# Tiles passed through memory in column blocks, with other queues and other places for the statistics, in a spectral and dense network on one core

## The chip, the core and the metric

One NeuronCore of a Trainium2 chip runs the whole program in one launch. It has five engines with a queue each: TensorE (PE, matrix products), VectorE (DVE), ScalarE (ACT), GpSimd (POOL) and SyncE (SP, which here only issues DMAs). DMAs can be issued from the queues of SyncE, ScalarE and GpSimd; a queue is worked off in order, so an issue that waits for a semaphore holds up all that stands behind it. The metric is the time on the device in microseconds (us).

## The reference

Four layers follow each other on a sequence of 2048 rows (tokens) with 1024 columns: A, B, A, B. Each one normalises its input along the columns and adds its result to it.

```python
def _layernorm(x, axis=-1, eps=1e-5):
    m = jnp.mean(x, axis=axis, keepdims=True)
    v = jnp.var(x, axis=axis, keepdims=True)
    return (x - m) / jnp.sqrt(v + eps)
...
    def _A_ref(x, w_r, w_i):
        X = rfft2(x)                      # over rows and columns, 2048 x 1024
        X = X * (w_r + 1j * w_i)
        return irfft2(X).astype(bfloat16)

    def _B_ref(x, w1, b1, w2):
        h = einsum("bsd,df->bsf", x, w1) + b1      # 1024 -> 3584
        act = h * tanh(softplus(h))                # Mish
        return einsum("bsf,fd->bsd", act, w2)      # 3584 -> 1024

    x = x + _A_ref(_layernorm(x), A_w_r, A_w_i)
    x = x + _B_ref(_layernorm(x), B_w1, B_b1, B_w2)
    x = x + _A_ref(_layernorm(x), A_w_r, A_w_i)
    x = x + _B_ref(_layernorm(x), B_w1, B_b1, B_w2)
```

## The kernel before, in words

The sequence stays in on-chip memory as 16 tiles of 128 rows (`XS`, tile `j` = rows `128 j` to `128 j + 127`). Layer A is written as products with tables of sines and cosines; its first stage (`s1`, matmuls at L635) wants the normalised sequence in another layout, `XR`: one partition for each pair of tile `j` and column block `h` (eight blocks of 128 columns), and in each partition 128 rows by 128 columns. Layer B computes both dense products with a scheme of seven block products instead of eight (Strassen's, in Winograd's form), for a pair of token groups at a time: tiles 0 to 7, and tiles 8 to 15.

A tracker turns reads and writes of named buffers into semaphore waits, and every engine executes its instructions in the order in which the program emits them. The order of the work is thus the order of the Python code; there is no scheduler. Buffers are places in one arena; a new buffer in an old place waits for the old one's readers and writers.

Layer B runs in this order, with the parts that matter here:

- The first dense product of tiles 8 to 15 is not finished when the first group's second product begins. `products(0, ...)` is the second product of the first half of the tokens. It has seven stages (n = 0 to 6), each a block product for four tiles (t = 0 to 3), at L1268; after each (n, t) the function `extra` is called. The two halves of a weight block lie in the slots `PB[n][k]`. Where the layer is not the last, five weight loads are issued just ahead of `products(0, ...)` (L1500, `load_w2`): three from SyncE's queue, two from GpSimd's. Differences of weight blocks (`w2_sum`, L1260) are made on VectorE out of pairs of these loads. `B21` is the second half of the block that stage 1 multiplies with (`PB[1][1]`).
- `stats_act(j)` takes the mean and the sum of squares of tile `j` on ScalarE, in two passes of L453 over 1024 columns. Where the layer is not the last, stages 5 and 6 of `products(0, ...)` each call it four times, for tiles 0 to 7 in all, whose new values stages 1 to 6 have just written (L1319).
- `quads(range(14), ...)` is the first dense product of the second half of the tokens: 14 passes of seven block products, 28 matmuls in a pass, at L1186. ScalarE copies the first of them out of PSUM (L574), VectorE adds others to that copy (L1191), and ScalarE applies Mish (L1196). Matmuls that go on accumulating in the bank of the first product wait for L574. The weights of pass n come from one of three slots; a slot is filled (`fill_slot`) from SyncE's queue when its pass is done, for passes 3 to 5 with four sums on GpSimd behind the load (L1081), for later passes from sums kept in memory (`w1s`). After each pass n, `after(n)` is called. It holds the arithmetic that turns sums into scales (`sums_to_mv`, `scales`, eleven small VectorE instructions), the normalisation of tiles 0 to 7 (`apply`, L524) and their stores to memory (`xn_store`), issued on GpSimd.
- `products(1, ...)` is the second product of the second half of the tokens. Its stages come in the order `BACK`, in which the last two stages finish tiles 8 to 11 (n = 5) and 12 to 15 (n = 6) one after the other. `extra` there normalises each finished tile and passes it on; at (3, 3), where the place of `XR` has become free, it issues the loads of tiles 0 to 7 (`xr_load`).
- After the last tile TensorE runs 24 matmuls without use (`spin`, L652), and layer A begins with `s1`, which needs all of `XR`'s first 64 rows of every tile before its first group (eight groups), and the rest before the ninth.

A normalised tile goes to `XR` in one of two ways. Through memory: `xn_store` writes the tile as it is (128 rows of 2 KB) to `xn_d[j]`, issued on GpSimd for tiles 0 to 7 and on ScalarE for 8 to 12; `xr_load`, on GpSimd, reads it back in runs of 256 B, so that the eight column blocks land on eight partitions. Directly: `xr_direct` copies each column block from on-chip memory to its partition, with one DMA for each block. Tiles 13 and 14 are copied with eight DMAs each, in turn from SyncE and GpSimd; tile 15 with sixteen (two halves of the rows), in turn from SyncE, GpSimd and ScalarE.

Of the kernel before, what the change touches and what calls it, by code (L numbers as in the profile page):

```python
# [7 lines left out]
P = 128  # L8
BF = dt.bfloat16
# [171 lines left out]
class KB:  # L181
# [123 lines left out]
    def build(self):  # L305
        nc = self.nc
        tabs = make_tables()
        con = {k: nc.inline_tensor(to_bf16_bits(v), name=f"c_{k.lower()}") for k, v in tabs.items()}
        self.con = {k: v.ap().bitcast(BF) for k, v in con.items()}
        self.con["IDF"] = nc.inline_tensor(np.eye(P, dtype=np.float32), name="c_idf").ap()  # L310
        self.u_d = nc.dram_tensor("u_scratch", (8, P, 16, P), BF, kind="Internal").ap()
        self.w_d = nc.dram_tensor("w_scratch", (8, P, 2, 2, 512), BF, kind="Internal").ap()
        self.w1s_d = nc.dram_tensor("w1s_scratch", (14, P, 3584), BF, kind="Internal").ap()
        self.w2s_d = nc.dram_tensor("w2s_scratch", (4, P, 14, 512), BF, kind="Internal").ap()
        self.xn_d = nc.dram_tensor("xn_scratch", (16, P, self.D), BF, kind="Internal").ap()
        from contextlib import ExitStack
        with ExitStack() as es:
            def sb(name, shape, dtype=BF):
                return es.enter_context(nc.sbuf_tensor(name, [P] + shape, dtype))

            sb("PAD0", [64])
            self.XS = sb("XS", [16, self.D])
            self.IDENT = sb("IDENT", [P])
            self.M = sb("M", [P])
            self.MT = sb("MT", [P])
            self.FD = sb("FD", [5 * 512])
            self.BD = sb("BD", [13 * P])
            self.B1 = sb("B1", [self.NF], F32)
            self.B1h = sb("B1h", [self.NF])
            self.BN = sb("BN", [16, 12], F32)  # L330
            self.MV = sb("MV", [16, 2], F32)
            self.RS = sb("RS", [4, 16], F32)
            self.EPS = sb("EPS", [32], F32)
            sb("PAD1", [32])
            self.PS = es.enter_context(nc.psum_tensor("PS", [P, 8, 512], F32))
            self.PSb = self.PS[:].bitcast(BF)
            self.arena_bytes = nc.sbuf_bytes_remaining // 64 * 64 - 64
            self.ARENA = es.enter_context(nc.sbuf_tensor("ARENA", [P, self.arena_bytes // 2], BF))
            self.r_bank = [Res(f"bank{i}") for i in range(8)]
            self.r_xs = [Res(f"XS{i}") for i in range(16)]  # L340
            self.r_mv = [Res(f"MV{i}") for i in range(16)]
            self.r_rs = [Res(f"RS{i}") for i in range(16)]
            self.r_ident, self.r_m, self.r_mt, self.r_fd, self.r_bd = (Res(n) for n in ("id", "m", "mt", "fd", "bd"))
            self.r_b1, self.r_eps, self.r_warm = Res("b1"), Res("eps"), Res("warm")
            self.r_ud = [Res(f"ud{i}") for i in range(8)]
            self.r_ud7 = [Res(f"udh{i}") for i in range(2)]
            self.r_wd = [Res(f"wd{i}") for i in range(8)]
            self.r_w1d = [Res(f"w1d{i}") for i in range(14)]
            self.r_w2d = [[Res(f"w2d{i}{k}") for k in range(2)] for i in range(4)]
            self.r_xnd = [Res(f"xnd{i}") for i in range(16)]  # L350
            self.npair = 0
            self.W1_OFF = self.arena_bytes - 4 * 4096
            self.layout()
            self.prologue()
            self.layer_A(0)
            self.layer_B(0, last=False)
            self.layer_A(1)
            self.layer_B(1, last=True)
            self.dma_wait_all()
            for p in (self.pe, self.dve, self.act, self.sp, self.pool):  # L360
                p.sem = es.enter_context(nc.semaphore(name=f"sem_{p.name}"))
            for d_ in self.dsems.values():
                d_.sem = es.enter_context(nc.semaphore(name=d_.name))
            self.block = es.enter_context(nc.Block())
            self.flush()

    def layout(self):
        K = 1024
        self.o = dict(XR=0, Z=0, X=12 * K, T=20 * K, YK=28 * K, V=40 * K, JT=48 * K, M0=49 * K, IDF=49 * K + 256, RT=50 * K,
                      JUNK=51 * K, WR=54 * K, YS=96 * K, UT=64 * K, MN=64 * K, Y=96 * K, XN=128 * K, U=128 * K,  # L370
                      FT=140 * K, BT=144 * K + 512, WT=self.W1_OFF)
        self.ob = dict(A=4 * K, XT1=60 * K, XT0=120 * K, XT2=104 * K, XT3=112 * K, W2=68 * K, JUNK=54 * K, TS=128 * K, XN2=140 * K,
                       SUMS=[0, 2 * K, 96 * K, 98 * K, 100 * K], P1=60 * K, X7=96 * K, W=120 * K, XN12=136 * K, JUNK2=0,
                       WS=self.arena_bytes - 21 * K)
        assert 149 * K <= self.W1_OFF and 144 * K <= self.ob["WS"], (149 * K, self.W1_OFF)

# [151 lines left out]

    def xn_store(self, j, b):
        b.unread = False  # L530
        prog = self.act if j >= 8 else self.pool
        self.dma(prog, self.xn_d[j], b.ap, f"xw{prog.name}{b.res.name[2:]}", reads=[b.res], writes=[self.r_xnd[j]])

    def open_xr(self):
        self.XR = self.alloc("XR", self.o["XR"], [P, P])
# [3 lines left out]
        self.r_xr = [halves[0], halves[0], halves[1], halves[1]]  # L539

    def xr_load(self, j):
        self.dma(self.pool, self.XR.ap[row_of(j, 0):row_of(j, 7) + 1:4, :, :], self.xn_d[j].rearrange("n (h l) -> h n l", l=P), f"xl{j % 4}",
                 reads=[self.r_xnd[j]], parts=self.r_xr[1:3])

    def xr_direct(self, j, b, parts, queues):
# [539 lines left out]
    def layer_B(self, li, last):  # L1085
# [411 lines left out]
        self.xn_buf = [self.alloc(f"XN{i}", self.ob["XN12"] + i * 2048, [self.D]) for i in range(2)] + self.xn_out  # L1497
        w2 = {}
        if not last:
            for name, k, slot, prog in (("B12", 0, "Q1", sp), ("B22", 0, "Q3", pool), ("B21", 1, "R0", sp), ("B12", 1, "Q2", pool),  # L1500
                                        ("B22", 1, "Q4", sp)):
                w2[slot] = load_w2(name, k, slot, prog)
            PB[1][1] = w2["R0"]
        else:
            load_b(STD, 1, 1)
            self.fill_slot(ws[2], 2)
# [28 lines left out]
        def extra(n, t):  # L1535
            if n == 0:
                self.stats_act(12 + t)
            if not last:
                own_sums(n, t)
            if (n, t) == (1, 3):  # L1540
                self.sums_to_mv(12, 4)
                self.scales(12, 4)
                normal(12)
                for j in (13, 14, 15):
                    xn[j] = self.apply(j)
            if (n, t) == (2, 2):
                for j in (13, 14, 15):
                    transposed(3, j - 12, xn[j], act, (6, 7, 0)[j - 13])
            turn(2)
            if (n, t) == (4, 3) and not last:  # L1550
                ws[2:] = self.open_slots("WS", self.ob["WS"], 2)
                self.fill_slot(ws[2], 2)
            if n > 4 and not last:
                self.stats_act(4 * n - 20 + t)
            if (n, t) == (5, 3):
                ws[0:2] = self.open_slots("WS", self.ob["WS"], 0, 1)
                for i in range(2):
                    self.fill_slot(ws[i], i)
                token_sums(1, last=False)
            if (n, t) == (6, 1):  # L1560
                B.update(token_sums(1))
        products(0, self.ob["WS"], STD, extra, last)
        order = [ws[n % 3] for n in range(14)]
        assert not turning
        stages = STD if last else BACK
        self.xn_out = self.xn_out + [self.alloc(f"XN{i}", self.ob["XN2"] + i * 2048, [self.D]) for i in range(2)]

        def after(n):
            if n + 3 < 14:
                self.fill_slot(order[n + 3], n + 3)  # L1570
            if 3 <= n < 7:
                load_b(stages, (n - 3) // 2, (n - 3) % 2)
            if not last:
                if n in (0, 3):
                    self.sums_to_mv(4 * (n // 3), 4)
                    self.scales(4 * (n // 3), 4)
                for j in ((), (0, 1), (2, 3), (), (4, 5), (6, 7))[n] if n < 6 else ():
                    self.xn_store(j, self.apply(j, out=True))
        quads(list(range(14)), order, B, after, lead)
        if not last:  # L1580
# [4 lines left out]
        def extra(n, t):  # L1585
# [8 lines left out]
            if n >= 5:  # L1594
# [1 line left out]
                self.stats_second(j, 0, False)  # L1596
                self.root(j, 1)
                b = self.apply(j, out=True)
                if j < 13:
                    self.xn_store(j, b)  # L1600
                if 8 < j < 14:
                    self.xr_load(j - 1)
                if j > 12:
                    self.xr_direct(j, b, j - 13 or 1, (sp, pool, act)[:2 + j // 15])
        products(1, self.ob["XT2"], stages, extra)
        if not last:
            self.spin(24, 7)
# [38 lines left out]
```

## Time and profile before

| what | value |
|---|---|
| time, median of 3 runs | 949.83 us (949.08 to 951.77) |
| span of the profiled execution | 949.6 us (its time 951.46 us) |
| mean granted TensorE clock | 0.982 |
| TensorE busy | 880.0 us, 93% |
| VectorE busy | 624.5 us, 66% |
| ScalarE busy | 429.1 us, 45% |
| GpSimd busy | 167.4 us, 18% |
| moved by DMA | 174.21 MB, mean 183 GB/s |

The profile is one execution. A line of a group or of the timeline names a source line (L453), the engine, the operation and what it writes and reads; a line of waits names who waited, for whom, how long in total, how often, and the longest. The clock is the share of full speed that the TensorE throttle granted. The first layer A and the first layer B fill the span up to about 490 us, the transition between B and the second A lies at 490 to 504 us, and the rest repeats A and B without a layer behind it. The edited parts lie at 229 us (weight loads), 293 to 362 us (statistics, normalisation and stores of tiles 0 to 7) and 454 to 504 us (loads of tiles 0 to 7, and tiles 8 to 15).

### The profile page before, as it was taken

Reading aid. Unit: us, or ns where it says so; the run is one execution under the profiler, and the core shown is the slowest. Engines: PE = TensorE matmul, PEld = TensorE weight load, DVE = VectorE, ACT = ScalarE, POOL = GpSimd, SP = SyncE. Lnnn points to the kernel's source line nnn. Section 1 sums busy time; section 2 is a strip of 40 time slices with the busy share of each in tenths; the row PEclk is TensorE's granted clock in tenths of the full one; section 3 lists DMA queues with packets and bytes.
Section 4 is the critical chain, followed back from the end, with each engine's and each line's share of the span. In section 5 each row is a group of like instructions: output and inputs, shape, how many; then the busy total and the mean of one; then the engine's idle time right before and its main releaser. Section 6 shows DMA issues by size and latency. Waiting matters only on the chain.

```text
span 949.6 us, 13503 instructions
## 1 busy us (share of the span) xinstructions
PE 880.0 (93%) x5473; PEld 471.9 (50%) x5473; DVE 624.5 (66%) x973; ACT 429.1 (45%) x623; POOL 167.4 (18%) x196
## 2 busy tenths in 40 slices
PE   0799699999999799999986996999999999999998
PEld 0577486444444344444435774864444444444443
DVE  7698468686789485557854874646846665555374
ACT  7798475457104655520006984845551005553000
POOL 3922004951005360010341200000000000000000
PEclk9999989999999899999998998999999999999999
DMA  9969853667775288354970697533245634831443
GB/s 287 275 212 303 206 132 128 224 235 196 263 252 182 100 287 343 112 199 155 213 170 17 203 223 195 181 106 115 87 145 175 215 144 155 303 125 60 172 132 114
DMA packets 149583, 174.21 MB, mean 183 GB/s; under 512 B 68480, under 2 KB 127952, under 8 KB 149520
## 3 DMA queue, kind: packets, MB, share of 16 engines
q1 hardware_dynamic: 134416, 123.83, 42.8%
q0 software_dynamic: 12208, 46.54, 14.9%
q10 hardware_dynamic: 2896, 2.97, 1.1%
q8 instruction: 43, 0.70, 0.3%
q14 instruction: 20, 0.16, 0.1%
HBM read 129.47 MB, written 40.37 MB: 179 GB/s over the span
## 4 chain that ended last, share of the span: by engine, by line
PE 75%; DMA 8%; DVE 8%; ACT 5%; SPq 1%; POOL 1%; issue 1%; ACTq 0%; DVEq 0%; POOLq 0%
PE PS L1268 29%; PE PS L1186 25%; PE PS L1148 9%; PE PS L799 2%; ACT ARENA L453 2%; PE PS L725 2%; PE PS L824 2%; PE PS L1020 2%; DMA ARENA<-w2s_scratch 1%; DMA ARENA<-in_B_w_dram 1%; PE PS L1109 1%; DMA ARENA<-c_bt 1%; DMA ARENA<-w1s_scratch 1%; SPq L250 1%; DMA ARENA<-u_scratch 1%
## 5 line engine op out<-in xcount | busy, mean ns | idle before, releaser
L1268 PE MATMUL PS<-ARENA 128*128 128x512 bf16 x1568 | 340.4, 379 | 2.0 <-DMA ARENA<-in_B_w_dram 1.9
L1186 PE MATMUL PS<-ARENA 128*128 128x512 f16 (+1 forms) x1232 | 270.8, 382 | 6.4 <-ACT ARENA L574 5.0
L1268 PEld LDWEIGHTS PS<-ARENA 128*128 128x128 bf16 x1568 | 153.2, 98 | 187.1 <-DMA ARENA<-in_B_w_dram 2.4
L1191 DVE TENSOR_TENSOR ARENA<-PS,ARENA 128x512 f32<-128x512 f32 x220 | 151.9, 691 | 99.2 <-PE PS L1186 90.9
L1186 PEld LDWEIGHTS PS<-ARENA 128*128 128x128 bf16 x1232 | 120.7, 98 | 155.2 <-ACT ARENA L574 5.4
L1196 ACT ACTIVATE ARENA<-ARENA,B 128x512 bf16<-128x512 f32 x132 | 95.2, 721 | 68.9 <-DVE ARENA L1191 62.6
L574 ACT ACTIVATE ARENA<-PS 128x512 f32<-128x512 f32 (+2 forms) x82 | 61.1, 745 | 118.7 <-PE PS L1186 95.8
L1148 PE MATMUL PS<-ARENA 128*128 128x256 bf16 (+1 forms) x576 | 87.6, 310 | 0.2
L1081 POOL TENSOR_TENSOR ARENA<-ARENA 128x512 bf16<-128x512 bf16 x56 | 71.5, 1277 | 81.0 <-DVE ARENA L524 59.9
L453 ACT ACTIVATE ARENA<-XS 128x1024 bf16<-128x1024 bf16 x52 | 54.8, 1054 | 41.3 <-DVE XS L1319 37.2
L1148 PEld LDWEIGHTS PS<-ARENA 128*128 128x128 bf16 x576 | 55.7, 99 | 27.1 <-DVE ARENA L1114 0.9
L1293 DVE TENSOR_TENSOR ARENA<-ARENA 128x3584 bf16<-128x3584 bf16 x32 | 63.9, 2017 | 0.0
L1319 DVE TENSOR_TENSOR XS<-PS,ARENA 128x512 bf16<-128x512 f32 x52 | 35.7, 689 | 38.6 <-PE PS L1268 38.2
L1152 ACT ACTIVATE ARENA<-PS,B 128x256 bf16<-128x256 f32 (+1 forms) x72 | 38.4, 542 | 36.1 <-PE PS L1148 35.7
L1311 DVE TENSOR_TENSOR ARENA<-PS,ARENA 128x512 f32<-128x512 f32 x48 | 33.0, 688 | 31.8 <-PE PS L1268 31.4
L1196 ACT ACTIVATE ARENA<-PS,B 128x512 bf16<-128x512 f32 x44 | 30.2, 687 | 19.1 <-PE PS L1186 19.1
L1307 DVE TENSOR_TENSOR ARENA<-ARENA,XS 128x512 f32<-128x512 f32 x52 | 36.7, 731 | 0.6
L1163 DVE TENSOR_TENSOR ARENA<-ARENA 128x2048 f16<-128x2048 bf16 x16 | 25.3, 1581 | 17.6 <-PE PS L1148 17.3
L799 PE MATMUL PS<-ARENA 128*128 128x256 bf16 x256 | 32.4, 273 | 4.2 <-DVE ARENA L788 3.2
L472 DVE BATCH_NORM_STATS2 BN<-XS 128x6 f32<-128x512 bf16 x52 | 32.7, 671 | 4.6 <-DMA XS<-in_A_x_dram 4.5
L777 ACT ACTIVATE ARENA<-PS 128x1024 bf16<-128x1024 f32 x32 | 33.4, 1074 | 4.5 <-PE PS L773 4.5
L444 ACT ACTIVATE RS<-MV,EPS 128x1 f32<-128x1 f32 (+2 forms) x11 | 3.3, 296 | 71.0 <-DVE MV L565 70.3
(98 smaller groups left out, 833.9 us busy)
## 6 DMA issues: line engine op xcount, KB each, us to landing
ARENA<-in_B_w_dram SPq DMA_DIRECT2D x30, 896.0 KB, 6.6
ARENA<-w1s_scratch SPq DMA_DIRECT2D x30, 896.0 KB, 4.7
ARENA<-w2s_scratch SPq DMA_DIRECT2D x24, 896.0 KB, 6.8
ARENA<-in_B_w_dram SPq DMA_DIRECT2D x26, 512.0 KB, 5.3
w1s_scratch<-ARENA POOLq DMA_DIRECT2D x14, 896.0 KB, 4.3
u_scratch<-ARENA SPq DMA_DIRECT2D x14, 512.0 KB, 3.4
ARENA<-u_scratch SPq DMA_DIRECT2D x14, 512.0 KB, 5.9
w2s_scratch<-ARENA POOLq DMA_DIRECT2D x8, 896.0 KB, 5.0
```

The source lines that it names most:

```text
L453: self.op(act, lambda e, i=i, f=f: e.activation(junk.ap, x, f, accum_out=sums[:, i:i + 1]), reads=[self.r_xs[j]], writes=[junk.res], parts ...
L574: fn = (lambda e: e.activation(dst, src, ACT.Copy)) if scale is None else \
L799: fns.append(lambda e, c=c, part=part: e.matmul(ps[:, c * 256:(c + 1) * 256], yk.ap[:, part, c * P:(c + 1) * P], t[:, (128, 0)[part]:(384, ...
L1081: self.op(self.pool, lambda e, dst=A(dst), x=A(x), y=A(y), op=op: e.tensor_tensor(dst, x, y, op), reads=[b.res] + list(after), writes=[b.rs])
L1148: fns.append(lambda e, db=db, bank=bank, fl=fl: e.matmul(PS[:, bank, 0:w], wb.ap[:, db, fl * P:(fl + 1) * P], x.ap[:, db, tok], start=(db ...
L1152: self.op(act, lambda e, bank=bank, ft=ft, at=at: e.activation(at[:, tok], PS[:, bank, 0:w], ACT.Mish, bias=self.B1[:, ft:ft + 1]), reads= ...
L1186: self.group([lambda e, db=db: e.matmul(PS[:, bank, :], A[:, db, :], mov[:, db, :], start=(start and db == 0), stop=(db == 3), skip_group_ ...
L1191: self.op(dve, lambda e: e.tensor_tensor(dst.ap, PS[:, bank, :], x.ap, ALU.add), reads=[self.r_bank[bank], x.res], writes=[dst.res])
L1196: self.op(act, lambda e: e.activation(at, src, ACT.Mish, bias=self.B1[:, ft:ft + 1]), reads=[res, self.r_b1], writes=[ra])
L1268: self.group([lambda e, i=i, k=k, b=PB[n][k].ap: e.matmul(PS[:, bank, :], ap[:, i, t * P:(t + 1) * P], b[:, i - 7 * k, :], start=(start an ...
L1293: self.op(dve, lambda e: e.tensor_tensor(ap[dst][:, f, :], ap[x][:, f, :], ap[y][:, f, :], op), reads=part(x, k) + part(y, k), writes=part ...
L1307: self.op(dve, lambda e: e.tensor_tensor(a[t], a[t], x, ALU.add), reads=[rx], writes=[r[t]])
```

## The change

The change has four parts; only the first layer B executes them, since the last one has no layer behind it.

1. The scratch `xn_d` is laid out by column blocks: for each tile, eight blocks of 128 rows by 128 columns. `xn_store` scatters a tile into it (1024 runs of 256 B) and is always issued on GpSimd. `xr_load` is issued on SyncE and reads eight runs of 32 KB, one for each partition of `XR`.
2. Tiles 13 and 14 go through memory, too: stores for tiles 8 to 14, and the load of tile j - 1 behind the store of tile j. Only tile 15 is copied directly, in two halves, in turn from GpSimd, ScalarE and SyncE.
3. The ScalarE statistics of tiles 0 to 3 move from stage 5 of `products(0, ...)` to stage 6, those of tiles 4 to 7 from stage 6 into `quads`, after passes 1 to 4. The scales of tiles 0 to 3 follow after pass 4 (before: 0), of 4 to 7 after pass 7 (before: 3); normalisation and stores of two tiles each after passes 5, 6, 8 and 9 (before: 1, 2, 4 and 5). The buffer into which ScalarE writes the values that nobody reads gets a place that is free in `quads` (`JUNK3`).
4. Of the five weight loads ahead of `products(0, ...)`, `B21` is issued first on SyncE (before: second, behind `B12`).

```diff
-        self.xn_d = nc.dram_tensor("xn_scratch", (16, P, self.D), BF, kind="Internal").ap()
+        self.xn_d = nc.dram_tensor("xn_scratch", (16, 8, P, P), BF, kind="Internal").ap()
...
     def xn_store(self, j, b):
         b.unread = False
-        prog = self.act if j >= 8 else self.pool
-        self.dma(prog, self.xn_d[j], b.ap, f"xw{prog.name}{b.res.name[2:]}", reads=[b.res], writes=[self.r_xnd[j]])
+        self.dma(self.pool, self.xn_d[j].rearrange("h n l -> n h l"), b.ap.rearrange("n (h l) -> n h l", l=P), f"xw{b.res.name[2:]}",
+                 reads=[b.res], writes=[self.r_xnd[j]])
...
     def xr_load(self, j):
-        self.dma(self.pool, self.XR.ap[row_of(j, 0):row_of(j, 7) + 1:4, :, :], self.xn_d[j].rearrange("n (h l) -> h n l", l=P), f"xl{j % 4}",
+        self.dma(self.sp, self.XR.ap[row_of(j, 0):row_of(j, 7) + 1:4, :, :], self.xn_d[j], f"xl{j % 4}",
                  reads=[self.r_xnd[j]], parts=self.r_xr[1:3])
...
-            for name, k, slot, prog in (("B12", 0, "Q1", sp), ("B22", 0, "Q3", pool), ("B21", 1, "R0", sp), ("B12", 1, "Q2", pool),
+            for name, k, slot, prog in (("B21", 1, "R0", sp), ("B12", 0, "Q1", sp), ("B22", 0, "Q3", pool), ("B12", 1, "Q2", pool),
                                         ("B22", 1, "Q4", sp)):
...
-            if n > 4 and not last:
-                self.stats_act(4 * n - 20 + t)
+            if n == 6 and not last:
+                self.stats_act(t)
...
+        self.junk = self.alloc("JUNK3", self.ob["JUNK3"], [self.D])
...
             if not last:
-                if n in (0, 3):
-                    self.sums_to_mv(4 * (n // 3), 4)
-                    self.scales(4 * (n // 3), 4)
-                for j in ((), (0, 1), (2, 3), (), (4, 5), (6, 7))[n] if n < 6 else ():
+                if 0 < n < 5:
+                    self.stats_act(3 + n)
+                if n in (4, 7):
+                    self.sums_to_mv(4 * (n // 7), 4)
+                    self.scales(4 * (n // 7), 4)
+                for j in {5: (0, 1), 6: (2, 3), 8: (4, 5), 9: (6, 7)}.get(n, ()):
                     self.xn_store(j, self.apply(j, out=True))
...
                 b = self.apply(j, out=True)
-                if j < 13:
+                if j < 15:
                     self.xn_store(j, b)
-                if 8 < j < 14:
+                if j > 8:
                     self.xr_load(j - 1)
-                if j > 12:
-                    self.xr_direct(j, b, j - 13 or 1, (sp, pool, act)[:2 + j // 15])
+                if j == 15:
+                    self.xr_direct(j, b, 2, (pool, act, sp))
```

## The prediction

> **What bounds the kernel now.** I read the page first: TensorE is busy for 93% of the span, and the chain that ended last is 75% TensorE. So time can only come from stretches in which TensorE stands still or runs at half clock. The waits of TensorE alone, asked in three windows that hold the edited code (200 to 312 us, 312 to 372 us, 455 to 530 us), give:
>
> ```profile
> PE PS L1268 <- DMA ARENA<-in_B_w_dram: 1.9, 1, 1.9
> ...
> PE PS L1186 <- ACT ARENA L574: 5.0, 1, 5.0
> PE PS L1186 <- POOL ARENA L1081: 0.9, 2, 0.6
> PE PS L1186 <- DMA ARENA<-w1s_scratch: 0.5, 1, 0.5
> ...
> PE PS L635 <- DMA ARENA<-ARENA: 9.0, 1, 9.0
> ```
>
> Each edit has one of these waits beside it. The timeline shows the second: ScalarE runs eight statistics passes (L453, two for a tile, tiles 4 to 7) before the first PSUM copy (L574) that TensorE needs.
>
> ```profile
> 307.50 1.06 ACT L453 ACTIVATE ARENA<-XS 128x1024 bf16<-128x1024 bf16 x1 [4.19 <-DVE XS L1319]
> ...
> 315.94 1.06 ACT L453 ACTIVATE ARENA<-XS 128x1024 bf16<-128x1024 bf16 x1
> 316.90 0.19 ACT L453 ACTIVATION_READ_ACCUMULATOR ARENA<-XS 128x1 f32 x1
> 317.18 0.60 ACT L574 ACTIVATE ARENA<-PS 128x512 f32<-128x512 f32 x1
> ```
>
> The windows view shows what follows that stall: 17 matmuls in 6 us at mean clock 0.57, where the steady loop needs 37/171 = 0.216 us for one at clock 1.00.
>
> ```profile
> 318.00:324.00 6.00, 6.00 (x17) 2.19 (x16) 1.99 (x3) 1.51 (x3) 0.00 (x0) 0.57 0.09 34
> 366.00:403.00 37.00, 36.55 (x171) 16.50 (x170) 20.75 (x30) 20.66 (x31) 0.00 (x0) 1.00 0.50 181
> ```
>
> The chain in order of time shows the third wait: tile 12's store, then GpSimd's queue (its load, and the block copies of tiles 13 to 15 stuck behind it), then the last copy's landing.
>
> ```profile
> 483.87 8.33 DMA xn_scratch<-ARENA
> 492.20 0.30 issue
> 492.50 6.48 POOL ARENA L251 x11
> 498.99 4.66 DMA ARENA<-ARENA
> 503.64 0.35 issue
> 503.99 3.59 PE PS L635 x32
> ```
>
> **What the Trainium skill says.** (1) "TensorE: Matmul & The Clock Gate", part 1 (the HAM clock gate): after about 3.4 us idle the array drops to half clock and needs about as long a busy window to return. The trace agrees: 5.0 us idle, then clock 0.57. (2) "DMA: Bandwidth & Descriptors", on why a DMA increments its semaphore by 16: the number of DMA engines follows the slowest dimension of both sides. The new load (8 rows by 16384) would get 8 of 16; the trace before has no such transfer. (3) Same page, Specifications: below 512 B a transfer is not at line rate (read-modify-write). The new store writes 256 B runs to memory; no store before does.
>
> **The change part by part.** Times are of the profiled span, 949.6 us; the unprofiled runs gave 949.08 to 951.77, so it can stand for them.
>
> *Weight load order (L1500).* SyncE issues B12 at 229.11 and B21 at 229.69; they land after 5.2 us (234.3) and 8.0 us (237.7). TensorE wants B21 at 235.85 and starts at 237.77. With B21 first it lands at about 234.3: 1.9 us saved. B12, now second, lands at 237.7, and VectorE, which waited for it until 234.37, starts its weight difference 3.4 us later. Behind it are two L1260, one L1293 and the first output add; the first product that needs such a difference is tile 0 of stage 2, at about 246.5 (248.4 less 1.9), with the halves ready at 239.8 and 244.6 by their 2.0 us rows. VectorE's idle of 1.2, 1.7 and 0.5 us at 257 to 265 takes up the backlog. Bounds: 0 to 1.9; taken 1.9.
>
> *Statistics.* Tiles 0 to 3 move by one stage in the program, but their inputs and ScalarE's free time are as before (they ran at 292.8 to 303.3), so they cost nothing new. Tiles 4 to 7 (4 x 2 passes, 9.6 us from 307.50 to 317.10) leave the place ahead of L574. The copy can then run at about 311.1, when its four matmuls (0.87 us from 310.13) are done, and TensorE, which stopped at 312.9, goes on. Removed: 5.0 us idle and the cold start. 17 matmuls warm take 3.7 us of those 6, and the last 5.5 us of cold clock held 13: 13 x 0.21 = 2.7 us. The smaller waits of that stretch, 0.9 (GpSimd) and 0.5 (w1s), come on top: 9.1 us can go.
>
> Against that stand new waits. GpSimd's sums for the second weight slot end at 314.9; TensorE would arrive at 310.13 + 20 x 0.217 = 314.5: 0.5. The slot chain stays tight: released 16 matmuls into a pass (3.5 us), load 3.8, sums 4.9 make 12.2 against two passes of 28 x 0.217 = 12.1; I leave 0.4. The four statistics now stand in passes 2 to 5 of the loop, ahead of the last Mish. ScalarE has 20.66 us of work in 37 us, 3.4 in a pass of 6.07; with 2.4 more it has 5.8, so it fits in rate, but each pass ends later, by about 0.5 us more each time, some 3.6 us in all. In pass 5 VectorE adds eleven scale operations (0.2 us each, 2.2 us), and the next PSUM bank may come free late. Bounds 0 and 3.6; I take 1.5. The stores of tiles 0 to 3 still fall beside the weight loads of passes 6 and 7 (from 350 to 372 us the DMA engines are full, at 394 GB/s), so the w1s wait of 0.5 stays. New waits: 0.5 + 0.4 + 1.5 + 0.5 = 2.9. Net 9.1 - 2.9 = 6.2 us, bounds 3.5 and 8.5. The doubled GpSimd issue of a scattered store (1.06 us, the row of the scattered load, against 0.54) lies where GpSimd has nothing else to do. SyncE's load of the FD table, and the second-product weights queued behind it, wait for these stores; the last goes out in pass 10 of 14, and its issue and landing (1.1 + 4.4 us) end before SyncE is through the last w1s load, so nothing is charged.
>
> *Loads of tiles 0 to 7, now on SyncE at 454.* SyncE is idle there until its w2s loads at 463.82, which landed late (12.4 us median) with scattered loads of 8 to 17 us before them. In 32 KB runs I expect that jam to go. It made TensorE lose 0.3 us (144 matmuls in 31.54 instead of 31.2). Saved 0.3.
>
> *Stores 8 to 14 and the last tile.* ScalarE loses five issues of 0.33 us, hidden. Tile 14's normalisation ends at 489.55. Its store goes out on GpSimd; the same 256 KB by that queue in 2 KB runs landed in 4.4 us at 341.6; the quickest store took 2.4, the slowest of this stage 8.3. Even a doubled data part (256 KB at 390 GB/s is 0.7 us) keeps it near 5, so I take 4.4: 494.0. SyncE waits for that, issues the load (0.4), and only then its five block copies of tile 15, about 0.7 each. The load: 32 KB per engine at 1/16 of 390 GB/s is 1.3 us, on the 1.7 us fixed that 2.4 less 0.7 leaves: lands about 497.4. SyncE's second copy of the first half is issued at 495.1 and lands (2.7 to 4.7 measured) by 498.6. GpSimd's third, 492.6 + 2 x 0.54, lands 4.6 later at 498.3. ScalarE's third, 492.6 + 2 x 0.75, lands 5.0 later at 499.1. TensorE starts at 499.1 instead of 503.99: 4.9 us, bounds 2 and 7. Idle from 494.95 stays above 3.4 us, so I give no credit for a warm start; the second half of the copies (by 501) is needed only after eight groups.
>
> Sum: 1.9 + 6.2 + 0.3 + 4.9 = 13.3; 949.6 - 13.3 = 936.3. What comes after (the transform, the last layer) is untouched and shifts.
>
> **The rivals.** (a) The end keeps its length: a store of 8.3 us, as tile 12's, puts the load's landing at 501.3 and SyncE's copies near 503. Then 949.6 - 8.4 = 941.2. For it: five such stores took 2.4 to 8.3 us. Against it: the slow ones ran beside the scattered loads that go. (b) The spread statistics stall TensorE as much in the loop as ahead of it: the 6.2 us vanish, 942.5. For it: 5.8 of 6.07 us. Against it: the loop has two PSUM sets, and the stall was one of first start. (c) Slower: 256 B writes to memory are so slow that stores queue. Tiles come every 3.05 us into four buffers, so beyond about 11.5 us of landing normalisation waits too. The start of the transform is 489.6 + 6.0 + landing, plus landing - 11.5; it loses more than the other 8.4 us from a landing of 14.3 us, 3.3 times the row I used. At 18 us: 7.4 us over that point, 957. Against it: one DMA then would run at 18 GB/s. (d) The edits only trade one wait for another at each place: 949.6.
>
> **How the numbers follow.** Forecast 936.3 (own range 932 to 940): 0.60; (a) 941.2: 0.16; (b) 942.5: 0.12; (c) 957: 0.08; (d): 0.04. Below 0.3% (2.8 us) a measurement of this kernel cannot tell a difference. Faster: 0.60 + 0.16 + 0.12 = 0.88; same 0.04; slower 0.08. To hold 8 in 10 the range takes in (a) and most of (b): 931 to 944.
>
> **What would show it.** Right: no wait on L574 near 312, no half clock at 318 to 324, the wait on in_B_w_dram gone, the transform's start 9 to 10 us (L635, after the spin) cut to about 4. Wrong: new TensorE waits in passes 5 to 7 of L1186 (b); stores of xn_scratch landing above 8 us (a), or VectorE waiting for them at L524 (c).

## The result, and the profile after

The changed kernel takes 936.89 us (median of 4 runs, 936.21 to 937.55); the kernel before, beside it, 949.46 us. The ratio is 0.9868, with a 95% interval of 0.9842 to 0.9895, so the change makes the kernel 1.3% faster. A later set of runs gave 937.76 against 950.78 us, 0.9856 (0.9838 to 0.9874). The forecast was 936.3 us. The profiled span fell from 949.6 to 934.9 us, by 14.7 us.

The waits of TensorE in the profile after, for the windows that now hold the edited code (200 to 312, 305 to 366, 360 to 450, 445 to 520 us), have two lines left that belong to the change:

```profile
PE PS L1186 <- POOL ARENA L1081: 0.3, 1, 0.3
...
PE PS L635 <- DMA ARENA<-ARENA: 6.5, 1, 6.5
```

The wait for `in_B_w_dram`, the one for L574 and the one for `w1s_scratch` are gone; the one at the transition has shrunk from 9.0 to 6.5 us. The windows view of the profile after (TensorE's busy time comes first, then the other engines, the granted clock and the DMA share) shows no half clock where it stood before:

```profile
318.00:324.00 6.00, 5.99 (x29) 2.55 (x28) 3.44 (x5) 4.56 (x7) 5.09 (x5) 1.00 0.30 89
```

There are 29 matmuls in the 6 us in which there were 17. The chain at the transition now runs over tile 14's store and SyncE's queue instead of GpSimd's:

```profile
475.77 0.56 DVE ARENA L524
476.33 0.66 issue
476.99 3.62 DMA xn_scratch<-ARENA
480.63 0.60 SPq L251
481.27 0.54 SPq L251
481.85 6.10 DMA ARENA<-ARENA
487.95 0.24 issue
488.19 5.29 PE PS L635 x48
```

The reader should see the order: tile 14's store lands 3.6 us after its issue, SyncE then issues tile 14's load (480.63) and its block copies of tile 15; the one issued at 481.85 lands last.

Where the 14.7 us come from is read off TensorE's timeline: the same seven events in both profiles, and the distance between each two.

| stretch of TensorE's work | before | after | difference | forecast |
|---|---|---|---|---|
| start to the first L1268 of this half | 220.36 | 218.51 | -1.85 | 0 |
| to the transposes (L1109) in stage 2 | 37.06 | 34.96 | -2.10 | -1.9 |
| to the first L1186 of `quads` | 52.71 | 52.71 | 0 | 0 |
| `quads`, to the first L1268 behind it | 92.85 | 83.86 | -8.99 | -6.2 |
| to the first matmul of `spin` (L652) | 86.63 | 86.33 | -0.30 | -0.3 |
| to the first L635 | 14.38 | 11.82 | -2.56 | -4.9 |
| L635 to the first L725 | 11.19 | 11.99 | +0.80 | 0 |
| from there to the end | 434.42 | 434.72 | +0.30 | 0 |

The first line lies ahead of every edit. A part of it is there early: the first matmul of L1020 starts at 112.93 us before and at 112.27 after. The other 1.2 us come behind it, and the clock differs there. In the windows view of 110 to 140 us, the end of the first layer A, of before and then of after, its mean is 0.83 and 0.89; in 30 us that is worth up to 1.8 us (an estimate).

```profile
110.00:140.00 30.00, 24.98 (x382) 21.85 (x381) 15.96 (x37) 19.70 (x27) 0.00 (x0) 0.83 0.49 125
```

```profile
110.00:140.00 30.00, 25.13 (x399) 22.41 (x398) 17.38 (x40) 20.93 (x30) 0.00 (x0) 0.89 0.53 140
```

So 1.85 us of the 14.7 come from code that no edit touches, in part from its clock. They differ from one execution to the next: in the 13 profiles of this case that same stretch took 218.5 to 223.3 us. This is why the readings below go by stretches where a microsecond or two matter.

### The profile page after: what moved, and what is told of

The parts are those of the page before. It is cut to its first block, busy times and chain, and to the rows that moved or that the text cites. A ratio compares the mean times of both kernels' runs of the same rounds, so it can differ in the third digit from the quotient of the medians.

```text
span 934.9 us, 13481 instructions
## 1 busy us (share of the span) xinstructions
PE 875.9 (94%) x5473; PEld 471.7 (50%) x5473; DVE 619.1 (66%) x973; ACT 427.5 (46%) x623; POOL 159.0 (17%) x183
## 4 chain that ended last, share of the span: by engine, by line
PE 83%; DMA 5%; DVE 5%; ACT 2%; SPq 2%; POOL 1%; issue 1%; DVEq 0%; ACTq 0%; POOLq 0%
PE PS L1268 35%; PE PS L1186 28%; PE PS L1148 9%; SPq L251 2%; PE PS L799 2%; PE PS L725 2%; PE PS L824 2%; PE PS L1020 2%; POOL ARENA L1081 1%; PE PS L1109 1%; DMA ARENA<-in_A_x_dram 1%; DMA ARENA<-c_bt 1%; DMA ARENA<-u_scratch 1%; DMA u_scratch<-ARENA 1%; PE PS L635 1%; ACT ARENA L641 1%
## 5 line engine op out<-in xcount | busy, mean ns | idle before, releaser
L1268 PE MATMUL PS<-ARENA 128*128 128x512 bf16 x1568 | 340.1, 379 | 0.0
L1186 PE MATMUL PS<-ARENA 128*128 128x512 f16 (+1 forms) x1232 | 267.8, 379 | 0.4 <-POOL ARENA L1081 0.3
L1268 PEld LDWEIGHTS PS<-ARENA 128*128 128x128 bf16 x1568 | 153.4, 98 | 184.5
L1186 PEld LDWEIGHTS PS<-ARENA 128*128 128x128 bf16 x1232 | 120.1, 98 | 146.8 <-POOL ARENA L1081 2.2
L574 ACT ACTIVATE ARENA<-PS 128x512 f32<-128x512 f32 (+2 forms) x82 | 61.1, 745 | 119.1 <-PE PS L1186 96.4
```

What stands on the lines that cost most here:

```text
L574: fn = (lambda e: e.activation(dst, src, ACT.Copy)) if scale is None else \
L1186: self.group([lambda e, db=db: e.matmul(PS[:, bank, :], A[:, db, :], mov[:, db, :], start=(start and db == 0), stop=(db == 3), skip_group_ ...
L1268: self.group([lambda e, i=i, k=k, b=PB[n][k].ap: e.matmul(PS[:, bank, :], ap[:, i, t * P:(t + 1) * P], b[:, i - 7 * k, :], start=(start an ...
```

## The experiments

**One part alone.** Three kernels carry one part of the change each, over the kernel before.

```diff
# w2_only
-            ... (("B12", 0, "Q1", sp), ("B22", 0, "Q3", pool), ("B21", 1, "R0", sp), ("B12", 1, "Q2", pool),
+            ... (("B21", 1, "R0", sp), ("B12", 0, "Q1", sp), ("B22", 0, "Q3", pool), ("B12", 1, "Q2", pool),
# stats_only: part 3 of the change (statistics, scales, apply and stores of tiles 0 to 7, JUNK3)
# mem_only: parts 1 and 2 of the change (layout, queues, tiles 13 and 14 through memory)
```

> The kernel before with B21 issued first, nothing else. My theory: TensorE's wait on in_B_w_dram near 236 us (1.9) goes and nothing takes its place, so the time falls by about 2 us (0.2%) and the distance from TensorE's first L1268 matmul of this half to the first matmul of quads shrinks by 1.9 to 2.1 us. Rival (only a shifted wait): VectorE's later weight difference stalls TensorE in stage 2 or 3 and that distance stays.

> The kernel before with the statistics, scales, normalisation and stores of tiles 0 to 7 at their new places; memory layout, queues and weight load order as before. Theory: this part alone gives the 9.0 us that the span of quads lost between the two profiles (first L1186 of the 14 passes to the first L1268 behind them), so about 940.5 us. Rival: a part of the 9 us came from the stores in other runs or from the moved weight load; then 942 to 945 us.

> The kernel before with the new layout, the new queues and tiles 13 and 14 through memory; statistics and weight load order as before. Theory: the stretch from the end of spin's first matmul to the first L635 shrinks by about 2.6 us, the wait for w2s_scratch near 479 us goes (0.3), so the time falls by about 3 us, to 946.5. Rival: the scattered stores, now beside the full DMA engines of passes 3 to 7, delay w1s loads and eat this; then no gain, 949.

| kernel | time, before beside it | ratio (95%) | to L1109 | `quads` | to L635 |
|---|---|---|---|---|---|
| before | | | 37.06 | 92.85 | 14.38 |
| w2_only | 948.71, 950.35 | 0.9983 (0.9972 to 0.9994) | 34.97 | 92.18 | 12.70 |
| stats_only | 941.38, 950.35 | 0.9905 (0.9891 to 0.9918) | 37.03 | 84.33 | 12.89 |
| mem_only | 949.80, 950.35 | 0.9990 (0.9977 to 1.0002) | 37.36 | 94.27 | 11.91 |
| changed | 936.89, 949.46 | 0.9868 (0.9842 to 0.9895) | 34.96 | 83.86 | 11.82 |

`w2_only` does what its theory said: the 2.1 us are there, and no later stage gives them back. `stats_only` carries the largest part: 9.0 us of time, 8.5 us of it in `quads`, nearer to its theory's 940.5 us than to the rival's 942 to 945. `mem_only` misses its 946.5: its interval includes no change. Two things are behind that. First, `quads` grew by 1.4 us. The waits of TensorE there (300 to 400 us):

```profile
PE PS L1186 <- ACT ARENA L574: 5.4, 1, 5.4
PE PS L1186 <- POOL ARENA L1081: 1.6, 2, 1.3
PE PS L1186 <- DMA ARENA<-w1s_scratch: 1.3, 2, 0.9
```

The waits for GpSimd's sums and for `w1s` were 0.9 and 0.5 us before. With the stores at their old places, GpSimd issues two scattered ones (0.9 us each instead of 0.54) ahead of the sums of the next weight slot, and the longest wait for these sums grew by as much, from 0.6 to 1.3 us. The rest of the 1.4 us is not shown to come from the stores: in `w2_only`, which has the old ones, TensorE waits 5.4 us for L574 and 0.9 us for `w1s`, too. In the changed kernel the stores come after the last sums, where nothing waits for GpSimd. So the new layout goes better with the new places of part 3. Second, the stretch to L635 in the old form is 12.7 and 12.9 us in the other two kernels and 14.38 only in the profile that the forecast was made from; five profiles of the new form (the changed kernel twice, `mem_only`, `lump` and `pairs`) give 11.6 to 12.3. By the means the transition is about 1.4 us shorter, not 2.6. The 0.3 us ahead of `spin` show no effect of the loads either: `w2_only` and `stats_only`, with the old loads, have the same 86.33 and 86.34 us there.

**Is it the place or the spreading?** All four statistics of tiles 4 to 7 after one pass:

```diff
-                if 0 < n < 5:
-                    self.stats_act(3 + n)
+                if n == 1:
+                    for j in range(4, 8):
+                        self.stats_act(j)
```

> The changed kernel with all four statistics of tiles 4 to 7 after pass 1 of quads and none after passes 2 to 4. ScalarE then has 9.6 us more in one pass of 6.07 us. Theory A (the gain comes from not standing ahead of the first copy; ScalarE catches up later): at most 1 us slower than the changed kernel. Theory B (the gain needs the spreading; a lump stalls TensorE because two sets of banks buffer less than one pass): a wait of TensorE on L574 or L1196 of 4 to 6 us in pass 2 or 3, about 941 to 943 us, half clock after it.

It took 945.07 us (0.9950, 0.9937 to 0.9964), and `quads` 91.76 us, 7.9 more than in the changed kernel. Its longest wait and its clock after the stall:

```profile
PE PS L1186 <- ACT ARENA L574: 4.6, 1, 4.6
```

```profile
333.00:338.00 5.00, 5.00 (x13) 1.83 (x14) 3.23 (x5) 2.45 (x4) 3.71 (x4) 0.53 0.15 59
```

Theory B holds, with a wait in its range and half clock behind it, though its 941 to 943 us were too low: standing behind the first copy is not enough, a lump of 9.6 us stalls TensorE by 4.6 us and costs another cold start. What the change gains here it gains by spreading.

**How much backlog is hidden?** Two tiles in each of two passes:

```diff
-                if 0 < n < 5:
-                    self.stats_act(3 + n)
+                if n in (1, 2):
+                    self.stats_act(2 + 2 * n)
+                    self.stats_act(3 + 2 * n)
```

> The changed kernel with two tiles' statistics after pass 1 of quads and two after pass 2. This asks why the backlog on ScalarE that my prediction charged with 1.5 us did not come. Theory A (instructions that follow each other on ScalarE overlap, so a pass without statistics fills less of it than its 3.4 us of listed durations, about 2.9; and the banks buffer about 5 us, as the lump of 9.6 us with its 4.6 us stall says): 4.8 us in the first such pass cause no stall; the backlog is then 4.8 - 3.1 + 4.8 = 6.5 us in the next, 1.5 us over the buffer: one wait on L574 of 1 to 2 us and about 1.5 us more than the changed kernel. Theory B (durations add up as listed, 3.4 + 4.8 = 8.2 in a pass of 6.07): backlog 4.8 - 2.7 + 4.8 = 6.9 over a buffer of 3.6 us: waits of 3 us and more. Theory C (ScalarE's late work doesn't reach TensorE below a whole pass): no wait at all.

941.96 us (0.9904, 0.9887 to 0.9922), `quads` 88.04 us. The first pair causes no wait, the second one:

```profile
PE PS L1186 <- ACT ARENA L574: 2.2, 1, 2.2
```

```profile
338.00:342.00 4.00, 3.77 (x12) 1.50 (x13) 3.08 (x5) 2.69 (x5) 0.57 (x1) 0.67 1.01 371
```

Theory A named a wait of 1 to 2 us, B 3 us and more, C none; 2.2 is nearest to A, a little above its range. The loss is 3.9 us beside the 84.19 of the same chip's changed kernel, not 1.5, as the short stall brought half clock with it (12 matmuls in 4 us).

**What ends the transition?** Three variants of the changed kernel.

```diff
# half_off_sp, in xr_direct
-                prog = queues[i % len(queues)]
+                prog = (self.pool, self.act)[h % 2] if k == 0 else queues[i % len(queues)]
# load_last, in extra
-                if j > 8:
+                if 8 < j < 15:
                     self.xr_load(j - 1)
                 if j == 15:
                     self.xr_direct(j, b, 2, (pool, act, sp))
+                    self.xr_load(14)
# eight, in extra
-                    self.xr_direct(j, b, 2, (pool, act, sp))
+                    self.xr_direct(j, b, 1, (pool, act, sp))
```

> The changed kernel with the first half of tile 15's copies (rows 0 to 63) issued alternately on GpSimd and ScalarE, four each, and only the second half in turn on all three. In the changed kernel the last copy of the first half that landed was SyncE's second, issued at 481.85 behind the load of tile 14 and landing 6.1 us later; the stretch from spin to the first L635 was 11.8 us. Theory A (SyncE's copies are late because they stand behind tile 14's load): the stretch falls to about 10.5 us. Theory B (small copies take 4 to 6 us whatever the queue, as the GpSimd and ScalarE ones did): it stays at 11.5 to 12.5.

> The changed kernel with the load of tile 14 behind SyncE's five copies of tile 15 instead of ahead of them. SyncE then doesn't wait for tile 14's store before it copies, but the load is issued some 1.5 us later. Theory A (copies behind the load): the copies land by about 485 in the changed kernel's times and the load, issued at 482.5 and landing 3 us or more later, decides: stretch 11 us. Theory B (copies slow in any queue): 12 us or more.

> The changed kernel with tile 15 copied by eight DMAs of 128 rows instead of sixteen of 64. Theory B (the number of small DMAs in flight sets their landing): fewer issues (two on SyncE, three on each of the others) land sooner, stretch from spin to L635 10.5 us. Theory A (behind the load): no gain, 11.5 to 12 us, since SyncE's second copy is still behind it.

Tile 14's store landed after 2.9 to 5.4 us in these executions, so the table gives the stretch from its landing, too. `spin44`, which comes last below, has the edit of `half_off_sp`.

| kernel | time (ratio) | `spin` to L635 | store's landing to L635 |
|---|---|---|---|
| changed | 936.89 (0.9868) | 11.82 | 7.58 |
| changed, once more | 937.76 (0.9856) | 12.31 | 7.7 |
| half_off_sp | 936.92 (0.9871) | 10.95 | 4.94 |
| spin44 | 935.90 (0.9850) | 11.32 | 7.8 |
| eight | 938.02 (0.9876) | 11.75 | 6.24 |
| load_last | 939.74 (0.9892) | 12.08 | 7.4 |

The chain of `half_off_sp` has no block copy in it any more; TensorE waits for the load itself:

```profile
479.75 5.38 DMA xn_scratch<-ARENA
485.14 4.63 DMA ARENA<-xn_scratch
490.08 3.45 PE PS L635 x32
```

Its 10.95 us lie between the 10.5 of theory A and the 11.5 of theory B. The store was the latest of the table there, after 5.4 us, and the copies of the first half had all landed before the load did. In `spin44` the store landed after 2.9 us, and the same queues ended otherwise, with a copy in ScalarE's queue, which holds no load:

```profile
481.77 0.69 ACTq L251
482.49 5.77 DMA ARENA<-ARENA
488.63 0.62 PE PS L635 x8
```

So theory A, that SyncE's copies are late because they stand behind the load in one queue, is not shown. The trace of the changed kernel speaks against it as well. The first two lines are copies being issued at 481.0 to 481.2 us in the two queues without a load, the third is SyncE's first copy, directly behind the load (481.2 to 481.5 us); the last number is the time to landing:

```profile
ARENA<-ARENA ACTq DMA_DIRECT2D x1, 16.0 KB, 6.1
ARENA<-ARENA POOLq DMA_DIRECT2D x1, 16.0 KB, 5.6
...
ARENA<-ARENA SPq DMA_DIRECT2D x1, 16.0 KB, 2.9
```

Theory B, late copies in any queue, fits this better, but not alone: the copies that `half_off_sp` issued before its load took 2.0 to 3.4 us. In the changed kernel those issued from 480.6 us on, around the load, took 2.5 to 6.1 us, with late ones in all three queues. Whether the load or the number of copies in flight makes them late stays open.

In `load_last`, whose 12.08 us are what theory B named, SyncE is held up by tile 13's store, which landed only at 482.49; after tile 13's load its five copies take until 486.4, so tile 14's load is issued 1.9 us after its store has landed (issue at 480.40, 4.1 us to landing) and lands another 5.2 us later. The wait has changed places and nothing is gained. `eight`, half as many copies of twice the size, gives 11.75 us and not the 10.5 of its theory B. The times of the three cannot be told from that of the changed kernel.

**Does the layout matter, or only the queues?** The changed kernel with the old layout:

```diff
-        self.xn_d = nc.dram_tensor("xn_scratch", (16, 8, P, P), BF, kind="Internal").ap()
+        self.xn_d = nc.dram_tensor("xn_scratch", (16, P, self.D), BF, kind="Internal").ap()
...                                       # xn_store, then xr_load
-        self.dma(self.pool, self.xn_d[j].rearrange("h n l -> n h l"), b.ap.rearrange("n (h l) -> n h l", l=P), ...
+        self.dma(self.pool, self.xn_d[j], b.ap, ...
-        ... self.xn_d[j], f"xl{j % 4}",
+        ... self.xn_d[j].rearrange("n (h l) -> h n l", l=P), f"xl{j % 4}",
```

> The changed kernel with the old memory layout (stores of 128 rows of 2 KB, loads of 1024 runs of 256 B), queues and everything else as in the changed kernel. Theory (the layout helps little: the gain of this part lies in the queues): stores land in 2.5 to 4.5 us, loads by SyncE cost at most 1 us more, stretch from spin to L635 within 1 us of 11.8, time within 1.5 us of the changed kernel. Rival (the long runs are what helps): loads of 256 B runs on SyncE's queue take twice as long, stretch 14 us or more and waits on w2s_scratch come back.

941.23 us (0.9904, 0.9878 to 0.9931), further from the changed kernel than the theory's 1.5 us. The stretch to L635 is not longer (10.77 us), against the rival; but the rival's other sign came:

```profile
PE PS L635 <- DMA ARENA<-ARENA: 5.4, 1, 5.4
PE PS L1268 <- DMA ARENA<-w2s_scratch: 3.2, 2, 1.9
```

TensorE waits 3.2 us for `w2s_scratch` in stage 6, and the stretch ahead of `spin` is 89.86 us instead of 86.33. The loads of tiles 0 to 7 stand ahead of those weights in SyncE's queue; in runs of 256 B they hold them up, in runs of 32 KB they don't. The issue itself is a large part of that. The eight loads on SyncE, in the old layout and then in the new one:

```profile
443.81 16.56 SPq L251 DMA_DIRECT2D ARENA<-xn_scratch  x8
...
440.72 5.24 SPq L251 DMA_DIRECT2D ARENA<-xn_scratch  x8
```

The weights are issued only behind them, at 460.41 instead of 450.88 us, in a kernel that was 3.1 us later at this place. That is the layout's use: not at the transition, but in making it harmless to put the loads on SyncE.

**Once more, and with a warm transform.** The changed kernel again (no edit), and `half_off_sp` with a longer `spin`:

```diff
-            self.spin(24, 7)
+            self.spin(44, 7)
```

> The changed kernel once more, beside the next two. Expected as before: about 937 us, stretch from spin to the first L635 of 11 to 12.5 us, passes of quads 83.8 to 84.5 us from the first L1186 to the first L1268 behind them.

> The kernel of half_off_sp (first half of tile 15's copies on GpSimd and ScalarE only) with 44 matmuls without use instead of 24 behind the last product, so that TensorE is busy until shortly before L635 begins. Theory (the transform's first stage runs at half clock since TensorE idled[...] before it, which costs 1 to 2 us there): the clock stays at 1.00, the stretch from the first L635 to the first L725 falls from 11.1 us to about 9.6, time 1.5 us below that of half_off_sp, some 935.5. Rival (that stage is bound by its PSUM copies on ScalarE and VectorE): no change, 11 us, or slower if the extra matmuls end after the data are there.

The changed kernel gave 937.76 us (0.9856, 0.9838 to 0.9874), `spin44` 935.90 us (0.9850, 0.9829 to 0.9872). The first stage of the transform after its first L635, `half_off_sp` and then `spin44`:

```profile
490.00:501.00 11.00, 9.39 (x128) 8.66 (x128) 8.30 (x7) 8.46 (x9) 0.00 (x0) 0.85 0.01 2
```

```profile
490.00:500.00 10.00, 8.27 (x122) 7.12 (x120) 7.38 (x7) 8.68 (x10) 0.00 (x0) 1.00 0.01 2
```

The clock stays at 1.00, and the stretch from L635 to L725 falls from 11.05 to 9.91 us, so the half clock at the start of the transform costs about 1.1 us in these two profiles. The whole time is not shown to be below that of the changed kernel: the two intervals overlap almost fully.

## Why the prediction was right

The forecast missed by 0.6 us. That it came so close is luck: the statistics gave 2.8 us more than forecast and the transition 2.3 us less, 1.1 us were lost behind it where the forecast had nothing, and 1.85 us of the profiled difference came from untouched code. What was right is the mechanism of the statistics and of the weight loads, and the direction at the transition.

*Weight load order.* Right: 2.10 measured, 1.9 forecast. `w2_only` shows it alone (2.09), and shows that VectorE's later difference takes nothing back.

*Statistics.* The mechanism was right: the stall on L574 and the half clock behind it went, and nearly nothing came in their place. The size was off: 8.99 us instead of 6.2 (7.8 to 9.0, as `quads` takes 92.2 and 92.9 us in `w2_only` and before, 83.9 to 84.4 in the eight profiles with all statistics at their new places). The term that failed is the 1.5 us for ScalarE's backlog in passes 2 to 5, with the 0.4 for the slot chain and the 0.5 for `w1s`; the 0.5 for GpSimd's sums came as 0.3. The profile after shows how little backlog there is. ScalarE's timeline, pass by pass:

```profile
322.07 1.04 ACT L453 ACTIVATE ARENA<-XS 128x1024 bf16<-128x1024 bf16 x1
...
328.30 1.04 ACT L453 ACTIVATE ARENA<-XS 128x1024 bf16<-128x1024 bf16 x1
...
334.46 1.04 ACT L453 ACTIVATE ARENA<-XS 128x1024 bf16<-128x1024 bf16 x1
...
337.25 0.59 ACT L574 ACTIVATE ARENA<-PS 128x512 f32<-128x512 f32 x1
337.73 0.72 ACT L1196 ACTIVATE ARENA<-ARENA,B 128x512 bf16<-128x512 f32 x1
...
340.65 1.04 ACT L453 ACTIVATE ARENA<-XS 128x1024 bf16<-128x1024 bf16 x1
```

The statistics begin 6.23, 6.16 and 6.19 us after each other, with a pass of 6.07: the backlog grows by 0.1 to 0.2 us a pass, not by 0.5. The forecast's 0.5 had no working: its own sum, 5.8 in a pass of 6.07, fits. The sum was high besides. From 328.30 to 334.46 us, in 6.16 us, the listed durations add up to 5.91 us and ScalarE's idle time to 0.82. The L574 line shows where the difference goes: a listed duration of 0.59 us, but the next instruction begins 0.48 us after. Instructions that follow each other without a wait overlap, so the sum of listed durations overstates a full engine. "ScalarE: Activation LUTs" of the Trainium skill says so in its section "What ACT_TABLE_LOAD costs": back-to-back activations overlap by about 93 ns; the distance here agrees (110 ns). How much slack there is, `pairs` shows: one pass hides a first 4.8 us of extra work, twice what the change puts into a pass, and a second 4.8 us brings a stall of 2.2.

*Stores of tiles 0 to 3 beside the weight loads.* Forecast as a remaining wait of 0.5 us, measured none. Their old places would have cost 0.7 us at GpSimd's sums (`mem_only`), which the forecast did not look at.

*Loads of tiles 0 to 7.* The 0.3 us were measured but not for the reason given: two kernels with the old loads have them too. `rows` shows the real stake, 3.5 us, which old layout and new queue together would have cost.

*The transition.* 2.56 us instead of 4.9 beside the one profile before, and about 1.4 us over all profiles. The 14.38 us before were the longest of three. The store was well sized: 3.6 us from its issue against 4.4, and the scattered stores of tiles 8 to 14 landed within 2.8 to 5.9 us. SyncE's second copy was issued at 481.85 us; the forecast's 495.1 less the 13.24 us by which `spin` had moved is 481.86. The term that failed is the landing of the block copies, in all three queues: SyncE's second took 6.1 us against the 3.5 forecast, GpSimd's third 5.6 against 4.6, ScalarE's third 6.1 against 5.0. The forecast read SyncE's landings as 2.7 to 4.7 us, but the profile before has longer ones of tile 15 (being issued at 493.9 to 494.0 us), with no load in their queue:

```profile
ARENA<-ARENA ACTq DMA_DIRECT2D x1, 16.0 KB, 7.2
ARENA<-ARENA SPq DMA_DIRECT2D x1, 16.0 KB, 6.8
```

The load lands after 4.6 us in `half_off_sp` and 5.2 in `load_last`, not 3.0. TensorE's wait came to 6.5 us, where about 4 was named as the sign of being right.

*The rivals.* (a), an end as long as before, was closest in kind: more than half of its gain failed to come, though through the copies and not through a slow store. Its sign, stores above 8 us, came only at tiles 0 to 3, where TensorE does not wait for them. (b) is excluded for the change as it is, and `lump` shows that it is true of the same work in one place. (c), the scattered stores backing up, is excluded: those of tiles 8 to 14 landed in 2.8 to 5.9 us, those of tiles 0 to 7 beside the weight loads in 3.6 to 8.2 (medians of two each), where the point from which it decides was 14.3. (d), no gain at all, is excluded by the time.

## What to carry to other kernels

9.6 us of work ahead of the first instruction of a loop stalled TensorE by 5.0 us here and brought a cold start. The same work stalled it by 4.6 us in one lump inside the loop, by 2.2 us in two portions, and not at all in four. To see whether an engine has room, compare the start times of its instructions in a full stretch, not the sum of their durations. A small DMA that decides when a stage begins should not stand behind an issue that waits for another DMA, and its landing should be priced from the longest on record: copies of one size in one queue took 2.7 to 6.8 us in one profile. One execution is a thin base, too: the stretch before had 14.4 us in one and 12.7 and 12.9 in others.

## What the runs showed of the hardware

A wait of 2.2 us was followed by half clock in `pairs` (clock 0.67 from 338 to 342 us), where the Trainium skill's page "TensorE: Matmul & The Clock Gate", part 1, names about 3.4 us of idle time. A wait as long, 2.2 us near 238 us in `mem_only`, had none behind it, and neither had the one of 1.9 us in the kernel before, as TensorE then ran 91 matmuls in 19.81 us. So the length of a wait alone did not decide it here. `mem_only`, behind its wait:

```profile
238.30:242.00 3.70, 3.59 (x16) 1.68 (x18) 2.22 (x3) 0.00 (x0) 0.00 (x0) 1.00 1.10 266
```

Stores of 256 KB in runs of 256 B, which its page "DMA: Bandwidth & Descriptors" (Specifications) puts below line rate, landed in 2.8 to 5.9 us (tiles 8 to 14), no later than those in runs of 2 KB (2.4 to 8.3 us in the kernel before). The latter ran beside the scattered loads that the change removes, so the two rows do not compare the forms alone. What the new form did cost was GpSimd's issue, 0.9 us (1.06 was taken) instead of 0.54. The new load of a tile shows as eight packets of 0.26 MB in all (DMA view of 481.2 to 481.5 us), which fits the eight engines of the forecast; the view does not name the engines.
